# One table of places for every operation after the first batch, in a packed-attention and SoLU kernel

## Chip, cores and metric

The kernel runs on one core of a Trainium2 chip. The metric is the time of one execution on the device, in microseconds (us). TensorE is PE in the profile, VectorE is DVE, ScalarE is ACT, GpSimd is POOL, and SyncE is SP; SP only issues DMA requests here. The weight loads of PE have a row of their own, PEld.

## The reference: what is computed

Inputs are q, k and v with 8 batches, 8 heads, 576 rows and 64 columns, and p with 32 packing rows per head. All is fp32.

```python
def sm_attn(qq, kk, vv):
    s = scale * np.matmul(qq, kk.transpose(0, 1, 3, 2))
    s = s - np.max(s, axis=-1, keepdims=True)
    a = np.exp(s)
    a = a / (np.sum(a, axis=-1, keepdims=True) + 1e-09)
    return np.matmul(a, vv)
p_packed = sm_attn(p, k, v)
out = sm_attn(q, p_packed, p_packed)
...
h = x @ w_in                       # x: 4608 tokens x 512; w_in: 512 x 1024
e = np.exp(h - h_max)
sm = e / (np.sum(e, axis=-1, keepdims=True) + 1e-09)
solu = h * sm
ln = (solu - mu) / np.sqrt(var + 1e-06) * g_ln
return (ln @ w_out).astype(np.float32)      # w_out: 1024 x 512
```

x is the attention's output with the heads of a token side by side. So each batch first attends from 32 packing rows to its 576 keys, then from its 576 queries to the 32 packed rows, and then every token goes through a two-layer block with a SoLU and a layer norm between.

## The kernel before

**A batch's attention** has two halves. `pack(b)` (line 317) turns the keys on DVE (kT, line 325; for batch 0 on PE), multiplies them with p (line 343, two steps r for the even and the odd heads, each into two PSUM banks `pa`), takes the row maximum on DVE (lines 346, 348), the exponential on ACT (line 356), turns the result on PE (line 372) with copies by ACT (e1T, line 373), multiplies by v (line 382), divides (pp, line 386), and turns that once more (ppT, lines 388 and 390). `unpack(b)` (line 401) works out the scale (lines 407 to 411), turns q (line 419 on DVE; for batches 0 and 1 `transpose_rows` does it on PE, lines 128 and 130, with ACT copies), multiplies with ppT (line 458), and does the softmax over blocks of 32: DVE blocks and sums (lines 430, 434, 439 to 441), POOL subtraction and product (lines 435, 442), ACT exponential (line 437). It never multiplies by the packed rows at once: it forms z = packed rows times w_in (line 474), splits it into two fp16 parts zh and zl (lines 476, 482), and splits the attention weights likewise into a2h and a2l (lines 486 to 489).

**A token tile** is 128 tokens; there are 36, four and a half to a batch, so that every ninth one takes 64 tokens of each of two batches (two groups of half-height matmuls side by side). `mlp_in` (line 492) makes h from three fp16 products, 12 matmuls of 512 columns into a two-bank tile `h` of which there are two (line 512), then the row maximum nm, the bound and the bias on DVE (lines 514 to 523), the exponential on ACT (line 524), and u = e * s_row * h on DVE (line 527), after which the bank pair is free. `mlp_norm` (line 530) takes the mean on POOL (line 535), writes the two fp16 parts of y on ACT and DVE (lines 537, 538), has a DMA turn them (yT, line 540), and sums the squares on ACT (line 542); POOL makes the row factor (lines 544 to 548). `mlp_out` (line 551) is 24 matmuls of 512 columns into a bank `po` (line 557), evicted by ACT with the row factor (line 559) and stored by SP (line 564).

**PSUM's eight banks** are four for h, two for `po` and two for `pa`.

**The order.** Batch 0's attention and the weights' conversion (lines 203 to 219 for both weights, 305 and 306 for w_out's two fp16 parts wch and wcl) are put in order by the framework's scheduler with hand-set priorities; so are all engines but PE throughout. From batch 1 on PE follows the order in which the program is written (`manual_schedule`, line 619): `step` (line 600) writes a tile's first product, pieces of the attention of the batch one or two ahead (`more`, line 628, with counts in FIRST_BATCH and LATER), and an earlier tile's second product. The attention comes in 3 to 12 slots of a batch's tiles. SP's requests stand in one queue: for batch b + 2 the keys (4 requests), the values (3) and the queries (16 requests from `load_blocks`, line 80; for batch 1 the 4 requests of `load_rows`) are issued at the first tile of batch b. There are three input buffers `raw` for k and q, and one for v. `keep_busy` (line 246) puts matmuls on ones into a `po` bank, 22 of them on PE before the first key.

Of the kernel before, what the change touches and what calls it, by code (L numbers as in the profile page):

```python
# [19 lines left out]
A_TOP = 15  # L20
LOW_BY = 'aaaaaaaa'
ZL_BY = 'pppp'
A2L_BY = 'pppp'
B0_BY = 'pppp'
PACK0 = [-350, 400, 2010, 365, -1000, 60, -2800, 200, 200]
W_IN = [110, -3000, 100, 20]
UNPACK0 = [-80, 350, -35, -110, -70, -25, 1965, 1025, 0]
W_OUT = [190, 20, -50, 3010]
SCALE_AT = -1060
CHUNKS = [6, 0, 7, 5, 1, 3, 4, 2]  # L30
PARTS = [100, -1160, -990, -200, -3010, -1050, 200, 200]
FIRST_BATCH = [[0, 0, 1, 1, 1, 2, 0, 2, 0, 2, 0, 0], [0, 1, 0, 0, 0, 4, 1, 1, 0, 0, 1, 1], [3, 0, 6, 0, 0, 0, 0, 0, 0, 0, 0, 0], [1000, 375], [0, -400, -50], 190]
LOADS = 'wpkwvwwqooPoo'
BUSY = [[8, 100], [6, 0], [0, -3000], [0, -100], [2, -190], [0, -485], [4, 200], [2, -2885]]
LATER = [[[4, 0, 1, 0, 0, 0, 0, 0, 0, 0, 1, 1], [0, 1, 0, 0, 1, 0, 0, 1, 0, 2, 3, 1], [0, 0, 0, 0, 0, 0, 0, 0, 0, 0, 0, 0], [1000, -200], [0, -110, -200], 0], [[3, 1, 0, 0, 0, 1, 0, 0, 1, 0, 0, 1], [0, 0, 0, 0, 1, 0, 1, 1, 0, 2, 3, 1], [0, 0, 0, 0, 0, 0, 0, 0, 0, 0, 0, 0], [975, -200], [0, -100, -200], 0], [[4, 0, 1, 0, 0, 1, 0, 1, 0, 0, 0, 0], [0, 0, 2, 0, 1, 0, 0, 0, 0, 4, 2, 0], [0, 0, 0, 0, 0, 0, 0, 0, 0, 0, 0, 0], [1000, -200], [0, -110, -200], 0]]
FETCH = [[['k', 0, 0], ['v', 0, 0], ['q', 0, 0]], [['k', 0, 0], ['v', 0, 0], ['q', 0, 0]], [['k', 0, 0], ['v', 0, 0], ['q', 0, 0]]]
# [5 lines left out]
def packed_attention_solu_kernel(ctx: ExitStack, tc: tile.TileContext, q: bass.AP, k: bass.AP, v: bass.AP, p: bass.AP, w_in: bass.AP, w_out: bass.AP, g_ln: bass.AP, out: bass.AP):  # L42
# [34 lines left out]
    ps_o = ctx.enter_context(tc.tile_pool(name='ps_o', bufs=2, space=PSUM))  # L77
    ps_a = ctx.enter_context(tc.tile_pool(name='ps_a', bufs=2, space=PSUM))

    def load_blocks(dst, src):  # L80


        blocks = src.rearrange('(g r) (a t) (e i) -> r e t g a i', r=2, t=32, e=2)
        for g in range(G):
            for r in range(2):
                for e in range(2):
                    c = 2 * r + e
                    nc.sync.dma_start(dst[32 * c:32 * c + 32, g], blocks[r, e, :, g])

    def load_k(src):  # L90


        raw = raws.tile([P, G, NB, 32], F32, name='raw', bufs=3)
        dst = raw.rearrange('p g a i -> p (g a) i')
        blocks = src.rearrange('h (a n t) (e i) -> n e t (h a) i', n=2, t=32, e=2)
        for n in range(2):
            for e in range(2):
                c = 2 * n + e
                nc.sync.dma_start(dst[32 * c:32 * c + 32], blocks[n, e])
        return raw  # L100

    def load_x(src):
        raw = raws.tile([P, G, NB, 32], F32, name='raw', bufs=3)
        load_blocks(raw, src)
        return raw
# [211 lines left out]
    def pack(b):  # L317
# [58 lines left out]
        for r in range(2):  # L376
            for c in range(NSC):
                n = P if c < 4 else LEFT
                for g in range(G):
                    h = 2 * g + r  # L380
                    at = (c // 2 * H + h) * 128 + c % 2 * D if c < 4 else 2048 + h * D
                    nc.tensor.matmul(pav[32 * g:32 * g + 32, r * D:(r + 1) * D], lhsT=e1T[:n, 2 * c + r, 32 * g:32 * g + 32], rhs=v_sb[:n, at:at + D], start=c == 0, stop=c == NSC - 1)  # L382
            yield
        pp = att.tile([P, 2, D], F32, name='pp')
        for r in range(2):
            nc.vector.tensor_scalar_mul(pp[:, r], pav[:, r * D:(r + 1) * D], rs[:, r:r + 1])
        ppt = ps_a.tile([P, 512], F32, name='pa')
        nc.tensor.transpose(out=ppt[:, :P], in_=pp.rearrange('p r d -> p (r d)'), identity=ident)
        ppT = att.tile([P, P], F32, name='ppT', bufs=2)
        nc.vector.tensor_copy(ppT, ppt[:, :P])  # L390
        peak = small.tile([P, 1], F32, name='peak')
        nc.vector.tensor_reduce(out=peak, in_=pp.rearrange('p r d -> p (r d)'), axis=AX.X, op=ALU.max, apply_absolute_value=True)
        nc.tensor.matmul(ppt[:, P:P + 1], lhsT=ones_f, rhs=peak, start=True, stop=True)
        packed[b] = (ppT, ppt)
# [6 lines left out]
    def unpack(b):  # L401

        qraw = loaded.pop(('q', b))
        ppT, ppt = packed.pop(b)
        unit = units[b] = small.tile([P, 4], F32, name='unit', bufs=4)
        power = small.tile([P, 1], F32, name='power')
        nc.vector.tensor_scalar(out=power, in0=ppt[:, P:P + 1], scalar1=w_bound, scalar2=2.0 ** (-40), op0=ALU.mult, op1=ALU.max)
# [13 lines left out]
        eng = nc.gpsimd  # L421
# [3 lines left out]
        def scores(bank, r, n):  # L425
            rows = slice(64 * r, 64 * r + 64)
            return [(bank[32 * g:32 * g + 32, :HALF], ppT[rows, 32 * g:32 * g + 32], qT[rows, g, n * HALF:(n + 1) * HALF]) for g in range(G)]
# [4 lines left out]
        def softmax(r):  # L432
            mx = small.tile([P, NB], F32, name='mx')
            nc.vector.tensor_reduce(out=mx, in_=s2[r], axis=AX.X, op=ALU.max)  # L434
            eng.tensor_tensor(out=s2[r], in0=s2[r], in1=mx.unsqueeze(2).broadcast_to([P, NB, J]), op=ALU.subtract)  # L435
# [6 lines left out]
            eng.tensor_tensor(out=w2, in0=w2, in1=sm.unsqueeze(2).broadcast_to([P, NB, J]), op=ALU.mult)  # L442
# [10 lines left out]
        else:  # L453
            for n in range(2):
                banks = pair(b)
                for both in zip(*(scores(banks[r], r, n) for r in range(2))):
                    for out_, lhsT, rhs in both:
                        nc.tensor.matmul(out_, lhsT=lhsT, rhs=rhs, start=True, stop=True)  # L458
                for r in range(2):
                    blocks(banks[r], r, n)  # L460
                if n == 0:
                    yield
            for r in range(2):
                softmax(r)
# [3 lines left out]
        for n in range(2):  # L468
            banks = pair(b)
            cols = slice(512 * n, 512 * n + 512)  # L470
            for g in range(G):
                for r in range(2):
                    rows = slice(64 * r, 64 * r + 64)
                    nc.tensor.matmul(banks[r][32 * g:32 * g + 32, :], lhsT=ppT[rows, 32 * g:32 * g + 32], rhs=w_in_sb[rows, g, cols], start=True, stop=True)  # L474
# [9 lines left out]
        for r in range(2):  # L484
            a2T = att.tile([P, NB, J], F32, name='s2', bufs=2).rearrange('p a j -> p (a j)')
            nc.vector.transpose(out=a2T, in_=a2[r].rearrange('p a j -> p (a j)'))
            hi, lo = (a2h[b % 2][:, r], a2l[b % 2][:, r])
            nc.scalar.copy(hi, a2T)  # L488
# [3 lines left out]
    def mlp_in(row, parts):  # L492

        h = ps_h.tile([P, DF], F32, name='h')
        m = P // len(parts)
        groups = []
        for x, (i, c) in enumerate(parts):
            rows, cols = (slice(m * x, m * x + m), slice(c, c + m))
            terms = []
            for r in range(2):  # L500
                terms += [(rows, a2h[i][:, r, cols], zh[i], r), (rows, a2h[i][:, r, cols], zl[i], r), (rows, a2l[i][:, r, cols], zh[i], r)]
            groups.append(terms)
        last = len(groups[0]) - 1
# [178 lines left out]
```

## Time and profile before

| what | value |
|---|---|
| runs shown | 468.38, 467.36 and 465.05 us, median 467.36 |
| the profiled execution's own time | 464.53 us |
| its span, first to last instruction | 462.8 us |
| PE busy, all matmuls | 413.4 us, 89% of the span |
| DVE, ACT, POOL busy | 318.9, 253.1 and 140.3 us |
| first matmul of the first token tile | 53.1 us |
| first matmul of a second product (line 557) | 84.7 us |
| first product of the last tile ends | 442.6 us |
| DMA | 67.0 MB, of 237,880 packets 208,912 under 512 bytes |

A group row reads: line, engine, operation, output<-inputs, shapes, count, then the busy time and the mean of one in ns, then how long the engine stood idle before them and what ended that. A row of windows gives for a stretch its length, each engine's busy time with the number of its instructions, the granted share of PE's clock, the share of time that the DMA engines were busy, and GB/s. A row of waits gives who waited for whom, the total in us, how often, and the longest. A row of the timeline gives the start, the length, and in brackets the idle time before it. Matmuls overlap, so that the mean of one is longer than the step from one to the next; the chain, which counts each stretch once, shows 12 matmuls of 512 columns in 2.6 us.

### The profile page before, as it was taken

Reading aid. Unit: us, or ns where it says so; the run is one execution under the profiler, and the core shown is the slowest. Engines: PE = TensorE matmul, PEld = TensorE weight load, DVE = VectorE, ACT = ScalarE, POOL = GpSimd, SP = SyncE. Lnnn points to the kernel's source line nnn. Section 1 sums busy time; section 2 is a strip of 40 time slices with the busy share of each in tenths; the row PEclk is TensorE's granted clock in tenths of the full one; section 3 lists DMA queues with packets and bytes.
Section 4 is the critical chain, followed back from the end, with each engine's and each line's share of the span. In section 5 each row is a group of like instructions: output and inputs, shape, how many; then the busy total and the mean of one; then the engine's idle time right before and its main releaser. Section 6 shows DMA issues by size and latency. Waiting matters only on the chain.

```text
span 462.8 us, 8369 instructions
## 1 busy us (share of the span) xinstructions
PE 413.4 (89%) x3117; PEld 186.2 (40%) x3122; DVE 318.9 (69%) x651; ACT 253.1 (55%) x424; POOL 140.3 (30%) x274
## 2 busy tenths in 40 slices
PE   9795477978379999989799999999999999999996
PEld 7471233422233453435333453344334534444442
DVE  2469898774738786978479768876797678564540
ACT  3698646733504763566345663765456737446451
POOL 0003911344015222531145222613244245212220
PEclk9989589999657999999999999999999999999999
DMA  8999999996386289945946479235324322345223
GB/s 291 374 260 302 231 170 160 221 208 119 51 192 113 68 152 208 177 114 101 211 103 124 120 156 182 68 92 150 92 45 121 87 69 69 88 117 133 73 74 108
DMA packets 237880, 67.00 MB, mean 145 GB/s; under 512 B 208912, under 2 KB 231440, under 8 KB 237328
## 3 DMA queue, kind: packets, MB, share of 16 engines
q1 hardware_dynamic: 237840, 66.48, 63.0%
q8 instruction: 24, 0.39, 0.4%
q14 instruction: 16, 0.13, 0.1%
HBM read 37.23 MB, written 9.44 MB: 101 GB/s over the span
## 4 chain that ended last, share of the span: by engine, by line
PE 43%; DVE 29%; ACT 8%; issue 7%; DMA 6%; POOL 5%; SPq 2%; DVEq 0%; ACTq 0%; POOLq 0%
PE po L557 20%; PE h L512 9%; DVE kT L325 4%; DVE yhl L538 4%; DVE nm L514 3%; DMA yT<-yhl 3%; PE pa L382 3%; DVE qT L419 3%; PE pa L458 2%; DVE u L527 2%; DVE mx L346 2%; DMA v_sb<-in_v_dram 2%; ACT yhl L537 2%; PE pa L372 2%; ACT e L356 2%
## 5 line engine op out<-in xcount | busy, mean ns | idle before, releaser
L557 PE MATMUL po<-wch,yT 128*128 128x512 f16 x576 | 180.8, 382 | 5.9 <-DMA yT<-yhl 5.8
L557 PEld LDWEIGHTS <-yT 128*128 128x128 f16 x864 | 82.3, 99 | 117.3 <-issue 16.5
L557 PE MATMUL po<-wcl,yT 128*128 128x512 f16 x288 | 109.7, 381 | 0.0
L524 ACT ACTIVATE e<-h,bias,unit 128x1024 f32<-128x1024 f32 x36 | 43.3, 1202 | 59.3 <-DVE bias L523 47.4
L538 DVE SCALAR_TENSOR_TENSOR yhl<-u,negmu,yhl 128x1024 f16<-128x1024 f32 x36 | 47.0, 1306 | 27.6 <-ACT yhl L537 26.9
L512 PE MATMUL h<-zh,a2h 128*128 128x512 f16 (+1 forms) x160 | 58.7, 393 | 7.6 <-ACT a2h L488 7.6
L527 DVE SCALAR_TENSOR_TENSOR u<-e,s_row,h 128x1024 f32<-128x1024 f32 x36 | 45.8, 1271 | 22.5 <-ACT e L524 21.9
L512 PE MATMUL h<-zh,a2l 128*128 128x512 f16 (+1 forms) x160 | 59.2, 390 | 0.8 <-POOL a2l L489 0.6
L537 ACT ACTIVATE yhl<-u,negmu 128x1024 f16<-128x1024 f32 x36 | 41.4, 1149 | 32.2 <-POOL negmu L535 31.9
L512 PE MATMUL h<-zl,a2h 128*128 128x512 f16 (+1 forms) x160 | 58.1, 390 | 0.0
L514 DVE TENSOR_REDUCE nm<-h 128x1 f32<-128x1024 f32 x36 | 43.8, 1216 | 12.6 <-PE h L512 12.1
L512 PEld LDWEIGHTS <-a2h 128*128 128x128 f16 (+1 forms) x320 | 28.6, 102 | 47.5 <-issue 11.4
L544 POOL TENSOR_SCALAR s_eps<-se,s_row 128x1 f32<-128x1 f32 x36 | 9.8, 272 | 106.6 <-ACT e L524 70.9
L542 ACT ACTIVATE e<-u,negmu 128x1024 f32<-128x1024 f32 x36 | 40.8, 1134 | 0.0
L559 ACT ACTIVATE o_sb<-po,c_row 128x512 f32<-128x512 f32 x36 | 24.4, 678 | 28.7 <-PE po L557 28.7
L547 POOL TENSOR_SCALAR c_row<-sq,k_out,s_eps 128x1 f32<-128x1 f32 x36 | 14.5, 404 | 80.8 <-ACT e L542 80.6
L476 ACT ACTIVATE zh<-pa,unit 128x512 f16<-128x512 f32 x28 | 17.8, 682 | 29.1 <-PE pa L474 28.5
L435 POOL TENSOR_TENSOR s<-s,mx 128x576 f32<-128x576 f32 x16 | 22.0, 1393 | 34.0 <-DVE mx L434 34.0
L430 DVE STREAM_TRANSPOSE s<-pa 128x288 f32<-128x288 f32 x28 | 12.0, 463 | 23.5 <-PE pa L458 23.5
L372 PE MATMUL pa<-ident,e 128*128 128x128 f32 (+1 forms) x80 | 15.8, 319 | 10.8 <-ACT e L356 9.1
L512 PEld LDWEIGHTS <-a2l 128*128 128x128 f16 (+1 forms) x160 | 15.7, 102 | 21.3 <-POOL a2l L489 3.2
L442 POOL TENSOR_TENSOR a<-a,sm 128x576 f32<-128x576 f32 x16 | 18.3, 1156 | 17.2 <-DVE bound L517 6.9
(121 smaller groups left out, 562.6 us busy)
## 6 DMA issues: line engine op xcount, KB each, us to landing
out_dram<-o_sb SPq DMA_DIRECT2D x36, 256.0 KB, 2.6
v_sb<-in_v_dram SPq DMA_DIRECT2D x16, 512.0 KB, 5.6
raw<-in_k_dram SPq DMA_DIRECT2D x28, 288.0 KB, 4.6
raw<-in_q_dram SPq DMA_DIRECT2D x96, 72.0 KB, 2.5
zh<-in_moe_w_in_dram SPq DMA_DIRECT2D x2, 1024.0 KB, 5.6
zl<-in_moe_w_in_dram SPq DMA_DIRECT2D x2, 1024.0 KB, 7.3
raw<-in_q_dram SPq DMA_DIRECT2D x4, 512.0 KB, 7.7
raw<-in_moe_w_out_dram SPq DMA_DIRECT2D x2, 1024.0 KB, 6.1
```

The lines of the kernel that those rows point to most:

```text
L325: nc.vector.transpose(out=kT[:, g], in_=kraw[:, g].rearrange('p a i -> p (a i)'))
L372: nc.tensor.transpose(out=pt[:n, i * P:(i + 1) * P], in_=e1[:, r, cols], identity=ident)
L435: eng.tensor_tensor(out=s2[r], in0=s2[r], in1=mx.unsqueeze(2).broadcast_to([P, NB, J]), op=ALU.subtract)
L512: nc.tensor.matmul(h[rows, 512 * n:512 * n + 512], lhsT=lhsT, rhs=z[:, r, 512 * n:512 * n + 512], start=t == 0, stop=t == last)
L514: nc.vector.tensor_reduce(out=nm, in_=h, axis=AX.X, op=ALU.max, negate=True)
L524: nc.scalar.activation(e, h, AF.Exp, bias=bias, scale=unit[:, 1:2], accum_out=se)
L527: nc.vector.scalar_tensor_tensor(out=u, in0=e, scalar=s_row, in1=h, op0=ALU.mult, op1=ALU.mult, accum_out=su)
L537: nc.scalar.activation(yhl[:, 0], u, AF.Identity, bias=negmu)
L538: nc.vector.scalar_tensor_tensor(out=yhl[:, 1], in0=u, scalar=negmu, in1=yhl[:, 0], op0=ALU.add, op1=ALU.subtract)
L542: nc.scalar.activation(e, u, AF.Square, bias=negmu, accum_out=sq)
L557: nc.tensor.matmul(po, lhsT=yT[:, a, c], rhs=w[:, c], start=c == 0 and t == 0, stop=c == NFC - 1 and t == 2)
L559: nc.scalar.activation(o_sb, po, AF.Copy, scale=c_row)
```

## The change

**One table for all engines.** `pack` and `unpack` stay for batch 0 alone. For batches 1 to 7 (`attention`) and all 36 token tiles (`token_tile`) each operation is registered with a place in tiles: a tile's number, or 4.5 times the batch's, plus a number from the tables TILE, ATT and MORE (MORE holds other numbers for odd batches, batch 1, and tiles 0 to 5 and 33 to 35). `perform` sorts them, takes the first whose predecessors are done and whose buffers are free by its own count, and `issue` ties each engine's instructions to the one before it, so that PE, DVE, ACT, POOL and SP all keep this order. `step`, `mlp_in`, `mlp_norm`, `mlp_out`, `prefetch`, FIRST_BATCH, LATER and FETCH are gone; their instructions are the same in the new functions.

**What else differs.** Four `raw` requests of a q (line 910 of the changed file), each with its own place, replace 16, for batch 1 too, whose q is now turned on DVE. The packed rows are turned twice, into a ppT with both halves of the partitions filled (pp holds each twice), so that a half of q's rows is one softmax step. The sum of their peaks is copied out of PSUM by ACT (`total`). `pa` has 3 banks and `po` 1. In batch 0 the softmax's two POOL operations per step go to DVE, and so does one of four zl and one of two a2l; q's load is ahead of w_in's last two; the 22 matmuls on ones before the first key are gone, and 12 stand about the turning of the packed rows.

```diff
-LOADS = 'wpkwvwwqooPoo'
...
+NPA = 3
+NPO = 1
+TILE = {'m1': -0.05,
...
+LOADS = 'wpkvwqwwooPoo'
...
+    def perform():
+        left, done = (sorted(plan, key=lambda x: x[:2]), set())
+        while left:
+            for n, (_, _, at, fn, args, after, takes, gives) in enumerate(left):
+                if all(x.lstrip('~') in done or x.lstrip('~') not in known for x in after) and all(free[x] >= takes.count(x) for x in takes):
+                    break
...
+            issue(fn, args)
...
+    def issue(fn, args):
+        n = len(seen)
+        fn(*args)
+        for ins in nc.cur_bb.bb.instructions[n:]:
+            if ins.engine in last:
+                tc.add_manual_dep(ins, last[ins.engine], mybir.DependencyInfo(mybir.DependencyClass.NoSync, mybir.DependencyReason.DATA), reason='order')
+            last[ins.engine] = ins.name
...
+        def load_part(name, c):
+            blocks = src.rearrange('h (a n t) (e i) -> n e t (h a) i', n=2, t=32, e=2)
+            nc.sync.dma_start(st[name].rearrange('p g a i -> p (g a) i')[32 * c:32 * c + 32], blocks[c // 2, c % 2])
...
+        at('ex', row_exp, after=['nm'], takes='e')
+        at('u', solu, after=['ex', 'bd'], takes='u', gives='h')
+        at('tr', y_turn, after=['yl'], takes='yT', gives='y')
+        at('m2a', second, 0, after=['tr'], takes='po')
+        at('m2b', second, 1, after=['m2a'], gives='yT')
+        at('ev', output, after=['m2b', 'cr'], takes='o', gives='po')
```

On PE the table spreads a batch's attention over about seven tiles: scores, turning, value product, second scores and z stand singly between halves of second products. The first three tiles' first products stand in a row, in the order tile 2, 1, 0, then all of batch 1's attention up to the value product, and then the first second product, tile 0's.

On SP, at the first transposing request of a token tile (line 540 before, 1213 now), the queue stood so before:

```order
L99 DMA raw<-in_k_dram 32x72x32 x4
L88 DMA raw<-in_q_dram 32x18x32 x16
L99 DMA raw<-in_k_dram 32x72x32 x4
L540 DMA_TRANSPOSE yT<-yhl 128x16x128
L88 DMA raw<-in_q_dram 32x18x32 x2
```

and stands so now:

```order
L910 DMA raw<-in_k_dram 32x72x32 x2
L910 DMA raw<-in_q_dram 32x72x32 x2
L918 DMA v_sb<-in_v_dram 64x8x64
L910 DMA raw<-in_q_dram 32x72x32 x2
L1213 DMA_TRANSPOSE yT<-yhl 128x16x128 x2
```

Batch 2's q and batch 3's keys stood ahead of the first two transposes; now batch 1's rest and one part of batch 2's q do.

On DVE, where batch 2's first scores meet their row maxima (mx, line 346 before, 945 now; nm is a token tile's maximum, bias frees its exponential; kT, qT the turned inputs, zl and s parts of batch 1's attention), it was:

```order
L346 TENSOR_REDUCE mx_979<-pa 128x1 x2
L348 TENSOR_REDUCE nmx<-mx_979 128x1
L357 TENSOR_REDUCE ssum<-es 128x1
L514 TENSOR_REDUCE nm<-h 128x1
L346 TENSOR_REDUCE mx_998<-pa 128x1 x2
L325 STREAM_TRANSPOSE kT<-raw 128x576 x2
L516 TENSOR_SCALAR bound<-nm,unit_1234 128x1
L523 TENSOR_SCALAR bias<-nm,unit_1234 128x1
L325 STREAM_TRANSPOSE kT<-raw 128x576 x2
L348 TENSOR_REDUCE nmx<-mx_998 128x1
```

and is now:

```order
L1177 TENSOR_REDUCE nm<-h 128x1
L1179 TENSOR_SCALAR bias<-nm,unit 128x1
L945 TENSOR_REDUCE mx_1080<-pa 128x1 x2
L947 TENSOR_REDUCE nmx<-mx_1080 128x1
L1079 STREAM_TRANSPOSE s_1085<-a_1015 128x576
L1185 TENSOR_SCALAR bound<-nm,unit 128x1
L1186 TENSOR_SCALAR bound<-nm,bound 128x1
L1188 RECIPROCAL s_row<-bound 128x1
L1198 SCALAR_TENSOR_TENSOR u,su<-e,s_row,h 128x1024
L926 STREAM_TRANSPOSE qT<-raw 128x576
L945 TENSOR_REDUCE mx_1129<-pa 128x1 x2
L947 TENSOR_REDUCE nmx<-mx_1129 128x1
```

The next batch's kT stood between the second maximum and the nmx that the exponential waits for; now nmx follows its maximum, and those four kT stand 23 rows later.

On ACT, at a token tile without attention beside it (e,se the exponential, yhl the high part, e,sq the squares, o_sb the eviction of an older tile's second product), it was:

```order
L524 ACTIVATE e,se<-h,bias,unit 128x1024
L537 ACTIVATE yhl<-u,negmu 128x1024
L542 ACTIVATE e,sq<-u,negmu 128x1024
L559 ACTIVATE o_sb<-po,c_row 128x512
```

and is now:

```order
L1193 ACTIVATE e,se<-h,bias,unit 128x1024
L1236 ACTIVATE o_sb<-po,c_row 128x512
L1206 ACTIVATE yhl<-u,negmu 128x1024
L1217 ACTIVATE e,sq<-u,negmu 128x1024
```

The eviction has moved up to stand right behind the exponential of a tile two numbers higher, ahead of that tile's yhl; the squares behind it are now those of the tile before.

More of the change, by code (lines that the diff above doesn't have):

```diff
@@ L20 @@
 A_TOP = 15
[L21 to L32, printed above, removed]
@@ L425, in scores @@
         def scores(bank, r, n):
[L426 to L427 removed]
+            x = n if halves else r
+            rows = slice(64 * x, 64 * x + 64)
+            return [(bank[32 * g:32 * g + 32, :HALF], ppT[rows, r, 32 * g:32 * g + 32], qT[rows, g, (r if halves else n) * HALF:][:, :HALF]) for g in range(G)]
         def blocks(bank, r, n):
@@ L453, in unpack @@
         else:
-            for n in range(2):
+            for x in range(2):
                 banks = pair(b)
-                for both in zip(*(scores(banks[r], r, n) for r in range(2))):
+                which = [(x, y) if halves else (y, x) for y in range(2)]
+                for both in zip(*(scores(bank, *at) for bank, at in zip(banks, which))):
                     for out_, lhsT, rhs in both:
                         nc.tensor.matmul(out_, lhsT=lhsT, rhs=rhs, start=True, stop=True)
-                for r in range(2):
[L460 to L464, printed above, removed]
+                for bank, at in zip(banks, which):
+                    blocks(bank, *at)
+                if halves:
+                    softmax(x)
+                if x == 0:
+                    yield
+            if not halves:
+                for r in range(2):
+                    softmax(r)
             yield
@@ L551, in mlp_out @@
-    def mlp_out(row, yT, c_row, mid=None):
-        po = ps_o.tile([P, DM], F32, name='po')
-        for c in range(NFC):
-            if c == NFC // 2 and mid is not None:
-                mid()
-            for t, (a, w) in enumerate(((0, wch), (0, wcl), (1, wch))):
-                nc.tensor.matmul(po, lhsT=yT[:, a, c], rhs=w[:, c], start=c == 0 and t == 0, stop=c == NFC - 1 and t == 2)
-        o_sb = mlp.tile([P, DM], F32, name='o_sb', bufs=2)
-        nc.scalar.activation(o_sb, po, AF.Copy, scale=c_row)
-        stores.append((out[row:row + P, :], o_sb))
@@ L657 @@
+    for b in range(1, B):
+        attention(b)
+    for i in range(B * S // P):
+        token_tile(i)
+    with tc.high_priority(offset=AHEAD) if AHEAD else nullcontext():
+        perform()
 _INS = ['q', 'k', 'v', 'p', 'moe_w_in', 'moe_w_out', 'moe_g_ln']
```

879 lines of the change are left out of this document (714 added, 165 removed).

## The prediction, made before the changed kernel ran

> **What bounds the kernel now.** I read the page's busy rows and slices first, then PE's windows by stage, then its waits, then the chain.
>
> ```profile
> PE 413.4 (89%) x3117; PEld 186.2 (40%) x3122; DVE 318.9 (69%) x651; ACT 253.1 (55%) x424; POOL 140.3 (30%) x274
> PE   9795477978379999989799999999999999999996
> PEclk9989589999657999999999999999999999999999
> ```
>
> PE is the busiest engine, and its slices are full from the fourteenth on; the holes, and the clock's, lie before. So I cut the span where PE's work changes: first product begins (53), second products begin (84.7), clock back at full (144.3), last first product ends (442.6).
>
> ```profile
> core 0: us, PE busy (x) PEld busy (x) DVE busy (x) ACT busy (x) POOL busy (x), PEclk, DMA share, GB/s
> 0.00:53.00 53.00, 37.48 (x382) 24.37 (x387) 33.03 (x54) 35.50 (x58) 11.27 (x17) 0.92 1.00 298
> 53.00:84.70 31.70, 25.83 (x239) 12.82 (x240) 27.67 (x56) 20.11 (x41) 10.29 (x19) 0.86 1.02 177
> 84.70:144.30 59.60, 45.56 (x350) 17.37 (x349) 37.67 (x81) 22.54 (x39) 17.92 (x31) 0.77 0.76 152
> 144.30:442.60 298.30, 288.85 (x2080) 124.93 (x2079) 216.18 (x456) 169.47 (x279) 98.92 (x204) 1.00 0.52 115
> 442.60:462.80 20.20, 15.64 (x72) 6.74 (x70) 4.39 (x8) 5.52 (x8) 1.93 (x6) 0.96 0.36 104
> ```
>
> In the long stage PE is idle for 298.3 - 288.9 = 9.4 us: no order can take more than that there. In the third, the handover from batch 0 to batch 1, it is idle for 14.0 of 59.6 us and slow besides. In the first two DMA is busy all the time and DVE for 27.7 of 31.7 us. What PE waited for in the third and in the fourth stage:
>
> ```profile
> PE pa L372 <- ACT e L356: 5.0, 1, 5.0
> PE po L557 <- DMA yT<-yhl: 2.9, 1, 2.9
> PE pa L382 <- ACT e1T L373: 2.0, 1, 2.0
> ```
>
> ```profile
> PE po L557 <- DMA yT<-yhl: 2.9, 2, 2.4
> PE pa L343 <- DVE zl L482: 2.3, 2, 1.2
> PE pa L458 <- DVE ppT L390: 1.9, 5, 0.4
> ```
>
> The 5.0 us are the place of the DVE excerpt above: nmx stood behind four kT, and ACT's exponential behind nmx. The clock follows such stops:
>
> ```profile
> 99.30:102.70 3.40, 1.09 (x5) 0.51 (x6) 3.40 (x7) 0.86 (x2) 0.89 (x2) 1.00 1.22 274
> 102.70:106.10 3.40, 3.40 (x9) 1.18 (x8) 1.87 (x5) 0.68 (x1) 1.75 (x2) 0.50 0.83 163
> 119.75:143.64 23.89, 16.56 (x151) 7.11 (x152) 14.31 (x34) 7.95 (x16) 4.92 (x11) 0.50 0.70 139
> ```
>
> A window in which PE worked for 1.09 of 3.40 us is followed by half speed, and after the 5.0 us it lasted 23.9 us. Half of 16.56 and of 3.40 busy us, 8.3 + 1.7, is lost so: the handover holds 59.6 - 14.0 - 10.0 = 35.6 us of work at full speed. These are the durations that I use:
>
> ```profile
> 216.25 1.73 PE pa L382 x80
> ...
> 386.79 2.59 PE po L557 x12
> ...
> 400.86 2.59 PE h L512 x12
> ...
> 442.57 1.24 DVE nm L514
> ...
> 449.72 3.71 DMA yT<-yhl
> ```
>
> ```profile
> L524 ACT ACTIVATE e<-h,bias,unit 128x1024 f32<-128x1024 f32 x36 | 43.3, 1202 | 59.3 <-DVE bias L523 47.4
> L538 DVE SCALAR_TENSOR_TENSOR yhl<-u,negmu,yhl 128x1024 f16<-128x1024 f32 x36 | 47.0, 1306 | 27.6 <-ACT yhl L537 26.9
> L527 DVE SCALAR_TENSOR_TENSOR u<-e,s_row,h 128x1024 f32<-128x1024 f32 x36 | 45.8, 1271 | 22.5 <-ACT e L524 21.9
> ...
> L559 ACT ACTIVATE o_sb<-po,c_row 128x512 f32<-128x512 f32 x36 | 24.4, 678 | 28.7 <-PE po L557 28.7
> ```
>
> ```profile
> L325 DVE STREAM_TRANSPOSE kT<-raw 128x576 f32<-128x576 f32 x28 | 19.8, 749 | 0.0
> ...
> L439 DVE TENSOR_REDUCE sm<-a 128x18 f32<-128x576 f32 x16 | 11.7, 740 | 0.3 <-ACT a L437 0.2
> ...
> L306 DVE SCALAR_TENSOR_TENSOR wcl<-yhl,gs,wch 128x512 f16<-128x512 f32 x4 | 4.7, 1220 | 0.8 <-ACT wch L305 0.8
> ...
> L306 DVE SCALAR_TENSOR_TENSOR wcl<-yT,gs,wch 128x512 f16<-128x512 f32 x4 | 2.8, 741 | 0.0
> ```
>
> **The change, part by part.** *First token tile.* DVE reached the first nm at 65.61:
>
> ```profile
> 65.61 1.21 DVE L514 TENSOR_REDUCE nm<-h 128x1 f32<-128x1024 f32 x1
> ```
>
> Six operations come to DVE (four of the softmax, a zl, an a2l). The trace has none on DVE; the bounds are 0 each, if DVE waited anyway, and the 1.31 of a 128x1024 row; I take the 0.74 of L439, of their width: +4.4. The four kT of batch 1 now stand behind this nm: -2.7. Four of wcl took 1.22, the other four 0.74, 0.48 less: up to -1.9. The matmuls on ones about the packed rows put these, and all behind, off by some 2 (12 at their cold step of 0.43, half covered). I take 67.5, with 64 and 71 as ends. From there the new order makes a chain, tile 1 first. DVE: nm and bias 1.4, the exponential's 1.3, u 1.3 (now h is free, and tile 0's first product, the third in PE's list, runs), yhl from 5.7 to 7.0 as in the profile's last chain, four kT 2.7, tile 0's nm 1.4, batch 1's maxima 1.0, u at 13.9, its yhl at 16.7, the second maxima 1.0; then ACT's exponentials 1.2, ten turnings and a copy at half speed 3.1, and the value product at half speed, 2.9. That is 24.9: the first second product can begin at 92.4, for 84.7 now. Tile 2's first product is then done, tile 3's (2.6) is not. Batch 1's q costs PE no transposes any more; those (5.4) lay in waits of this stage and give nothing.
>
> In the Trainium skill's "TensorE: Matmul & The Clock Gate" (What's actually happening) the clock falls after an idle window of about 3.4 us. Here a window a third busy did it, so the measurement decides; by the page's rule alone the stops of this chain need not halve the clock, and the sum would be some 4 us less.
>
> *Handover.* 35.6 + 2.6 = 38.2 us of work. I laid the new lists of PE, DVE and ACT beside each other with these durations; PE stops for ppT (0.5, and 0.6 for batch 2), for `pa` banks of batch 1's second scores and z until DVE has read them (0.2, 0.95, 0.9, and 0.8 at batch 3's scores), for the second scores of batch 2, whose bank ACT's exponential frees behind a tile's (1.3), and for e1T (0.6): 5.9. Half speed for the first half of tile 0's second product: 1.3. With 14.0 as now it would be 8 more, with none 6 less. It ends 45.4 after 92.4: 137.8.
>
> *Long stage.* Its work is 288.9; the second turning of the packed rows adds 0.1 each, 0.8 in all with its copies hidden on DVE and ACT (busy 72% and 57% here). Nine tiles with two batches, laid out likewise from tile 9 on, give PE stops of 0.4 (ppT), 1.15 (scores, bank), 0.3 (z, bank) and some small ones: 2.7 for 9 tiles, against 98.0 - 92.8 = 5.2 now:
>
> ```profile
> 163.00:261.00 98.00, 92.81 (x720) 39.77 (x718) 73.88 (x160) 54.61 (x92) 33.08 (x65) 1.00 0.73 146
> ```
>
> Two and a half such periods have attention in them: 6.8, with 0 and 13 as ends. So 296.5. The single `po` bank costs nothing here: between two second products PE has a first product (2.6), and the eviction (0.68) stands behind an exponential that is over by then, unless DVE lags by more than 4 us.
>
> *SP.* The 16 requests of a q took 9.54, four of the same size 5.25:
>
> ```profile
> 72.81 5.25 SPq L99 DMA_DIRECT2D raw<-in_k_dram  x4
> ...
> 121.71 9.54 SPq L88 DMA_DIRECT2D raw<-in_q_dram  x16
> ```
>
> The packets are the same, so DMA is not relieved; only a transpose behind them lands sooner. The 2.9 + 2.9 us of PE's waits for yT are what that can be worth, and they are in the idle times above. Batch 1's q as 128-byte pieces falls in the stage where DMA is full; its last part waits for the kT to free a buffer and is wanted 9 us later: nothing.
>
> *Tail.* Three second products follow the last first product. The third eviction from the end now stands behind the last tile's exponential and yhl, 1.1 us after its product, and the next one costs 0.85; the 0.6 wait for yT is covered by that. 20.2 becomes 21.2 (20.2 to 22.2).
>
> **Sum.** 92.4 + 45.4 + 296.5 + 21.2 = 455.5 for 462.8, and 1.7 around it (464.53 - 462.8): 457. The three runs of before lie at 465.05 to 468.38, the profiled one half a us under them, so a run of after may come out up to 4 over the sum.
>
> **The rivals.** *Nothing is left to wait for:* the first nm as early as now (-2), half of the handover's stops (-3), none in the long stage (-6.8): 445. For it: DVE is busy for 73.88 of 98.0 us, and a spread attention asks for less at a time. Against: DVE's list is fixed, and its u and yhl rows show 22.5 and 27.6 us of waits. *The handover's loss comes back elsewhere:* one stop that drops the clock costs 8.3 as at 119.75: 465, no change. For it: my chain has two stops of 4 us for PE before 92. *DVE's order becomes the bound, slower:* per tile it has 73.88 / 9 = 8.2 us of work and waits of (22.5 + 27.6) / 36 = 1.4; PE's pace is 10.6. From 1 us more of waiting per tile, DVE sets the pace; at 2 us more, 1 us per tile over the 22 tiles left: 479. For it: pp, ss and zl now stand in the list as single places, each behind PE or ACT. Against: my nine tiles, where they waited for 2.3, 0.7 and nothing.
>
> Another way to be slower is in the skill's section on a second failure mode (psum-queue depth-cycling), same page: micro-stops between groups with cycled PSUM banks make the clock oscillate. Here stops of up to 2.4 us left it at 1.00 through 298 us; it is in the slower case with 0.02.
>
> That the order isn't kept is no rival: the lists are the program.
>
> **How the numbers follow.** Forecast (449 to 463) 0.45, nothing left to wait for 0.24, no change 0.18, slower 0.13. About 1% can be told from no change. Faster by over 1% is below 462.7: the second case and nearly all of the first, 0.68; same 0.19; slower 0.13. The range reaches to the rivals' middles without the slowest: 443 to 469; the forecast's own is 449 to 463.
>
> **What would show it.** Right: the first nm at 66 to 69, the first second product at 90 to 95, half speed before it and none after 105; PE idle under 4 us per nine tiles from 140 on; no PE wait over 2 us there. Wrong: second products before 86 or after 98; DVE without idle time in the long stage; PE waits for `po`.

## The result, and the profile after

The changed kernel takes 434.58 us (median of 4 runs, 432.99 to 435.57), the kernel before 467.87 beside it (465.05 to 468.69): a ratio of 0.9295, 95% interval 0.9242 to 0.9348. The direction was forecast; the size, 457, and the range, 443 to 469, were not: the kernel is 8 us faster than the range's lower end. The profiled execution has a span of 431.9 us. Of the kernel with PE and SP alone tied (below) one execution took 801.08 us beside 476.74 to 482.78 in three others; it is not explained, and the ratio given for that kernel leaves it out.

The busy row and two slices of the profile after:

```profile
PE 388.8 (90%) x3053; PEld 179.5 (42%) x3053; DVE 331.3 (77%) x662; ACT 247.7 (57%) x422; POOL 135.3 (31%) x268
...
PE   7697075499999999999999999999999999999985
...
PEclk9999668699999999999999999999999999999999
```

From the ninth slice on PE is full, but for the last two, and its granted clock (PEclk, in tenths) stays at full. PE's windows of the changed kernel, cut at the same events as before: first product begins (56.0), second products begin (87.8), the fourth second product begins (127.9), the last first product ends (410.2); then nine tiles of the long stage, and the two middle stages as one:

```profile
core 0: us, PE busy (x) PEld busy (x) DVE busy (x) ACT busy (x) POOL busy (x), PEclk, DMA share, GB/s
56.00:87.80 31.80, 19.74 (x159) 8.82 (x160) 25.06 (x45) 17.45 (x32) 6.78 (x14) 0.71 0.51 91
87.80:127.90 40.10, 38.34 (x347) 17.00 (x344) 33.87 (x78) 20.91 (x38) 14.39 (x26) 1.00 0.90 174
127.90:410.20 282.30, 279.55 (x2104) 124.43 (x2103) 230.13 (x471) 169.05 (x286) 104.15 (x207) 1.00 0.64 137
410.20:431.90 21.70, 15.84 (x72) 6.84 (x70) 4.51 (x8) 6.27 (x10) 3.37 (x10) 1.00 0.46 110
...
170.20:259.10 88.90, 88.19 (x719) 39.52 (x718) 75.83 (x160) 54.02 (x94) 33.83 (x67) 1.00 0.81 159
...
87.80:410.20 322.40, 317.89 (x2450) 141.43 (x2447) 264.00 (x548) 189.96 (x324) 118.55 (x232) 1.00 0.68 142
```

| | before | forecast | after |
|---|---|---|---|
| first nm | 65.6 | 67.5 | 64.0 |
| first second product begins | 84.7 | 92.4 | 87.8 |
| handover, to the fourth second product | 59.6 | 45.4 | 40.1 |
| long stage | 298.3 | 296.5 | 282.3 |
| tail | 20.2 | 21.2 | 21.7 |
| span | 462.8 | 455.5 | 431.9 |

Of the miss of 23.6 us 4.6 lie ahead of the first second product, 5.3 and 14.2 in the two middle stages, and the tail gives 0.5 back. All that PE still waits for between 87.8 and 410.2:

```profile
PE pa L1010 <- DVE ppT L1007: 3.5, 5, 0.9
PE pa L940 <- DVE s L1035: 0.6, 1, 0.6
PE pa L1028 <- DVE s L1035: 0.2, 1, 0.2
```

To see where the 35 us of these stages went, I take both as one stretch, from the start of the first second product to the end of the last first product. Before, its row is this:

```profile
84.70:442.50 357.80, 334.31 (x2427) 142.28 (x2426) 253.82 (x535) 192.00 (x318) 116.75 (x235) 0.96 0.56 122
```

Length less PE's busy time is idle time: 23.5 before, 4.5 after. From the records I also add the steps from each matmul of the attention to the next matmul, without the idle time that the trace shows, apart for the stretches at half speed. Before, 20.2 us of steps of all kinds lie at half speed, so 10.1 are lost; after, almost none. The attention's steps come to 64.3 us before, with those at half speed counted half, and to 56.8 after. So 35.4 is 19.0 of idle time, 10.1 of half speed and 7.5 of the attention's steps, less about 1 in the steps of the two products (one first product more, 2.6, lies in the stretch after). The last part was a surprise: the matmuls are the same, but for one more turning. By line it is the second scores that fell most, from 15.8 us (line 458) to 9.4 (line 1028); the first scores fell by 1.7, the turning of e by 1.7, and z rose by 1.2. The table, used for the experiments too, holds one profiled execution of each kernel; the attention column counts half speed in full, and for the kernel before with 3 + 1 banks it holds 1.7 of matmuls on ones, which write an attention bank there:

| kernel | stretch begins | its length | PE idle in it | attention's steps |
|---|---|---|---|---|
| before | 84.7 | 357.8 | 23.5 | 70.6 |
| after | 87.8 | 322.4 | 4.5 | 56.8 |
| after, 2 + 1 banks | 93.4 | 354.0 | 20.1 | 67.0 |
| after, 2 + 2 banks | 92.2 | 353.4 | 19.6 | 67.2 |
| before, 3 + 1 banks | 93.7 | 343.4 | 20.3 | 61.5 |
| after, PE and SP tied | 94.7 | 357.5 | 27.4 | 62.2 |
| after, PE, SP and DVE tied | 90.5 | 326.0 | 5.9 | 56.9 |
| after, groups split | 88.5 | 332.0 | 4.7 | 66.1 |
| after, control of that | 88.8 | 323.5 | 3.9 | 58.5 |
| before, PE tied | 84.6 | 361.9 | 28.3 | 69.8 |

### The profile page after: what moved, and what is told of

The parts are those of the page before. It is cut to its first block, busy times and chain, and to the rows that moved or that the text cites. A ratio compares the mean times of both kernels' runs of the same rounds, so it can differ in the third digit from the quotient of the medians.

```text
span 431.9 us, 8093 instructions
## 1 busy us (share of the span) xinstructions
PE 388.8 (90%) x3053; PEld 179.5 (42%) x3053; DVE 331.3 (77%) x662; ACT 247.7 (57%) x422; POOL 135.3 (31%) x268
## 4 chain that ended last, share of the span: by engine, by line
PE 75%; DVE 10%; ACT 5%; issue 4%; SPq 3%; DMA 2%; POOL 1%; ACTq 0%; DVEq 0%
PE po L1232 41%; PE h L1173 19%; PE pa L1066 4%; PE pa L991 3%; PE pa L940 2%; PE pa L974 2%; PE pa L1028 2%; DVE u L1198 2%; DMA zh<-in_moe_w_in_dram 2%; SPq L449 1%; ACT yhl L1206 1%; DVE yhl L1209 1%; SPq L441 1%; DVE nm L1177 1%; PE pa L581 1%
## 5 line engine op out<-in xcount | busy, mean ns | idle before, releaser
L1173 PE MATMUL h<-zh,a2h 128*128 128x512 f16 (+1 forms) x160 | 56.4, 391 | 12.1 <-ACT a2h L835 7.8
L1209 DVE SCALAR_TENSOR_TENSOR yhl<-u,negmu,yhl 128x1024 f16<-128x1024 f32 x36 | 45.6, 1265 | 23.7 <-ACT yhl L1206 23.7
L1173 PE MATMUL h<-zh,a2l 128*128 128x512 f16 (+1 forms) x160 | 55.9, 387 | 0.3 <-POOL a2l L836 0.3
L1173 PE MATMUL h<-zl,a2h 128*128 128x512 f16 (+1 forms) x160 | 55.9, 387 | 0.0
L1206 ACT ACTIVATE yhl<-u,negmu 128x1024 f16<-128x1024 f32 x36 | 41.3, 1147 | 19.6 <-POOL negmu L1202 19.2
L1202 POOL TENSOR_SCALAR negmu<-su 128x1 f32<-128x1 f32 x36 | 6.8, 190 | 89.0 <-DVE u L1198 84.9
L1224 POOL TENSOR_SCALAR c_row<-sq,k_out,s_eps 128x1 f32<-128x1 f32 x36 | 15.7, 436 | 47.4 <-ACT e L1217 46.0
L1094 POOL TENSOR_TENSOR a2l<-s,a2h 128x576 f16<-128x576 f32 x14 | 18.8, 1343 | 29.4 <-ACT a2h L1090 29.4
L1042 POOL TENSOR_TENSOR s<-s,mx 128x576 f32<-128x576 f32 x14 | 17.2, 1227 | 26.5 <-DVE mx L1039 26.5
L1055 POOL TENSOR_TENSOR a<-a,sm 128x576 f32<-128x576 f32 x14 | 18.6, 1332 | 19.6 <-DVE sm L1052 19.6
L955 ACT ACTIVATE e<-pa,nmx 128x288 f32<-128x288 f32 x28 | 13.7, 494 | 19.1 <-DVE nmx L947 19.1
L1046 ACT ACTIVATE a<-s 128x576 f32<-128x576 f32 x14 | 9.5, 682 | 24.6 <-POOL s L1042 24.6
```

The lines of the kernel that those rows point to most:

```text
L1055: nc.gpsimd.tensor_tensor(out=st['a2', r], in0=st['a2', r], in1=st['sm', r].unsqueeze(2).broadcast_to([P, NB, J]), op=ALU.mult)
L1094: nc.gpsimd.tensor_tensor(out=lo, in0=a2T, in1=hi, op=ALU.subtract)
L1173: nc.tensor.matmul(h[rows, 512 * n:512 * n + 512], lhsT=lhsT, rhs=z[:, r, 512 * n:512 * n + 512], start=t == 0, stop=t == end)
L1206: nc.scalar.activation(st['y'][:, 0], st['u'], AF.Identity, bias=st['negmu'])
L1209: nc.vector.scalar_tensor_tensor(out=st['y'][:, 1], in0=st['u'], scalar=st['negmu'], in1=st['y'][:, 0], op0=ALU.add, op1=ALU.subtract)
```

## The experiments

Times are medians, ratios are to the kernel before beside the same runs (the changed kernel's own is 0.9295).

### Is it the third attention bank?

In two kernels the bank counts of the changed kernel are other ones: two for the attention and two for the second product, as before; then two and one, so that the attention's count alone differs. `perform` counts free banks, so that it also places some operations later: with two and one banks, of the order of lines that PE worked through, 190 of 206 entries stand as they did, and of DVE's 477 of 522.

```diff
-NPA = 3
-NPO = 1
+NPA = 2
+NPO = 2
```

> The changed kernel with two banks for the attention and two for the second product, as before (the table is the same; the planner moves the few rows that do not fit). Theory 'the third attention bank took the bank waits away': PE waits for DVE to read scores and z, about 1 us per batch and more at the handover: 440 to 448. Rival 'the banks do not matter, the order does': 434 to 437.

> The changed kernel with two attention banks in place of three and one bank for the second product, as it has now (seven of the eight banks used). Theory 'the third attention bank is what the table needs': as with two and two, 463 to 472. Rival 'it was the second bank of the second product that moved the order for the worse': 434 to 442.

Measured: 467.54 (ratio 1.0024, 0.9992 to 1.0056) and 466.91 (1.001, 0.9981 to 1.0038). The whole gain is gone with one attention bank less, far more than the 440 to 448 that I had expected of the first kernel, and whether the second product has two banks or one makes no difference beside it. Of the 37.2 us by which the span grew 5.7 lie ahead of the first second product. PE's windows and waits of the kernel with two and one:

```profile
93.40:447.40 354.00, 333.95 (x2450) 144.89 (x2447) 265.31 (x547) 189.59 (x324) 113.88 (x232) 0.97 0.62 129
...
141.30:144.70 3.40, 1.45 (x17) 0.31 (x16) 3.23 (x11) 0.66 (x2) 0.73 (x3) 1.00 0.82 163
144.70:151.50 6.80, 6.18 (x40) 1.81 (x39) 4.34 (x11) 2.43 (x6) 2.36 (x3) 0.50 0.45 93
```

```profile
PE pa L1066 <- ACT e L955: 6.4, 2, 3.2
PE pa L1028 <- DVE s L1035: 3.6, 4, 1.7
...
PE pa L1066 <- ACT e1T L981: 2.3, 3, 1.3
PE pa L940 <- DVE s L1035: 1.8, 3, 0.6
```

The rows of waits name what PE waits for: a bank that ACT's exponential or its copy, or DVE's transpose, has not read yet. z (line 1066) stands in PE's list between other operations' banks, and with two of them it stands until one is read. Behind a window with 1.45 busy us of 3.40, the clock is at half for 6.8. And the timeline of PE shows what such a wait does to a group of eight matmuls that needs two banks:

```profile
167.78 1.04 PE L1066 MATMUL pa<-w_in_sb,ppT 64*32 64x512 f32 x2
170.14 1.09 PE L1066 MATMUL pa<-w_in_sb,ppT 64*32 64x512 f32 x14 [1.32 <-ACT e1T L981]
```

Each fp32 matmul has two records. The first of the eight found its bank free and ran alone for 1.04 us; the other seven waited 1.32 more, and then took 1.09 together, as long as all eight take in a row. So the wait cost 1.32 of idle time and some 1.04 that the profile counts as busy.

Then the other way round: the kernel before with three attention banks and one for the second product, nothing else of the change (its matmuls on ones write an attention bank).

```diff
-    ps_o = ctx.enter_context(tc.tile_pool(name='ps_o', bufs=2, space=PSUM))
-    ps_a = ctx.enter_context(tc.tile_pool(name='ps_a', bufs=2, space=PSUM))
+    ps_o = ctx.enter_context(tc.tile_pool(name='ps_o', bufs=1, space=PSUM))
+    ps_a = ctx.enter_context(tc.tile_pool(name='ps_a', bufs=3, space=PSUM))
```

> The kernel before with three banks for the attention and one for the second product, and nothing else of the change (the matmuls on ones write an attention bank). Theory 'the third attention bank is the gain by itself': PE's bank waits and the pairs that stood apart go as they did in the changed kernel, some 20 us or more less, 440 to 450. Rival 'the third bank is worth something only with lists that use it': the old lists have kT, sums and maxima in places that make DVE late anyway, and the single bank of the second product now waits for its eviction: 462 to 472.

Measured: 461.73 (0.9895, 0.9859 to 0.993). Neither number: a little is gained. The table tells why: the stretch is 14.4 us shorter, but begins 9.0 later and leaves a tail of 24.5 for 20.3. The late start lies in batch 0: the first product of a token tile begins at 62.1 for 53.1, behind a wait of 11.5 us for a2h that was 6.2. In the stretch PE now waits for the second product's bank:

```profile
PE po L558 <- ACT o_sb L560: 6.7, 5, 1.8
PE po L558 <- DMA yT<-yhl: 5.9, 4, 2.4
```

Of the stretch, the bank alone takes 14.4, the table alone (two and one banks) 3.8, both 35.4; of the whole time they take 5, nothing and 33. Most of the gain needs the two together. Why batch 0 came later is open.

### Which engines' lists?

The same table, but only some engines are tied to it, and the scheduler orders the rest.

```diff
         for ins in nc.cur_bb.bb.instructions[n:]:
+            if ins.engine not in (mybir.EngineType.PE, mybir.EngineType.SP):
+                continue
             if ins.engine in last:
```

> The changed kernel with only PE and SP tied to the table's order; the scheduler orders DVE, ACT and POOL. Theory 'the fixed lists of DVE, ACT and POOL took the waits away': PE's idle time of 0.7 us per nine tiles goes back towards the 5.2 of before, some 13 us over the long stage, and the first 88 us change too: 445 to 460. Rival 'PE's order alone does it': within 2 us of 434.6.

> The same kernel as with PE and SP alone tied, for a profile to read: 477 to 483; the theories differ in the place: if the scheduler's order of DVE is at fault, PE's idle time ends at DVE's nm, maxima and transposes, if ACT's, at its exponentials and evictions.

> The changed kernel with PE, SP and DVE tied to the table's order; the scheduler orders ACT and POOL alone. Theory 'DVE's list is the one that matters', since most of PE's waits end at DVE: 434 to 442. Rival 'ACT's list matters as much' (the eviction ahead of yhl, the exponentials): 455 to 485, as with PE and SP alone (482).

Measured: 482.45 with PE and SP alone (median of all four; 1.0274, 1.0198 to 1.0349), slower than before by 2 to 3.5%; 476.8 in the execution whose profile stands below; 440.38 with DVE tied too (0.9428, 0.9395 to 0.9461). DVE's list, added to those of PE and SP, is worth 36 to 42 us, and those of ACT and POOL on top of it 5.8. The windows of PE's stretch and its waits with PE and SP alone, then the windows with DVE tied too:

```profile
94.70:452.20 357.50, 330.08 (x2449) 143.86 (x2446) 256.98 (x539) 187.34 (x320) 116.26 (x228) 0.97 0.60 128
```

```profile
PE pa L1068 <- ACT e L957: 4.7, 2, 2.4
PE pa L942 <- ACT e L957: 4.6, 1, 4.6
PE pa L942 <- DVE s L1037: 4.2, 1, 4.2
PE pa L1030 <- DVE s L1037: 4.0, 3, 2.5
PE po L1234 <- ACT o_sb L1238: 3.6, 3, 2.2
```

```profile
90.50:416.50 326.00, 320.06 (x2449) 141.63 (x2446) 262.68 (x543) 188.81 (x322) 120.40 (x230) 1.00 0.67 140
```

The place is again a bank that waits for a reader, in the last row the second product's: line 957 is the attention's exponential, which stands behind DVE's maxima, line 1037 DVE's transpose of the second scores. With DVE in the table's order 27.4 us of idle time become 5.9. In these runs three banks are enough only where DVE reads them in the order in which PE fills them.

### What is a group of eight worth?

A transposing matmul of the unit matrix, into columns that nothing reads, behind the first of the eight matmuls of each second-score group; as a control, the same one behind the eighth.

```diff
                     nc.tensor.matmul(bank[y][32 * g:32 * g + 32, :HALF], ...)
+                    if g == 0 and y == 0:
+                        nc.tensor.transpose(out=bank[y][:, HALF:HALF + P], in_=ident, identity=ident)
```

> The changed kernel with one transposing matmul of the unit matrix (128 columns, into columns of the same bank that nothing reads) put behind the first of the eight quarter matmuls of each second-score group, 14 groups in all. Theory 'whole groups': the eight run side by side and cost 0.65 us together, the first one alone costs 0.60 (the rows of before at 176.88 and 221.16), so each group grows by 0.60 and the added 0.12: 14 x 0.72 = 10 us, nearly all on PE's path, 444. Rival 'PE has slack': the group's cost is hidden and only the added matmul counts or nothing does: 434.6 to 436.5.

> The control: the same transposing matmul, but behind the eighth of each group, so that the groups stay whole. Theory 'whole groups': 14 x 0.12 = 1.7, so 436.3. Rival 'an added matmul with a wait costs as much wherever it stands': as the split kernel, 444.

Measured: 443.32 (0.9486, 0.9433 to 0.9538) and 435.9 (0.932, 0.9282 to 0.9359), 8.7 and 1.3 over the changed kernel, where 10 and 1.7 were expected. The split itself is the difference, 7.4 us or 0.53 for each of 14 groups; the attention's steps differ by 66.1 - 58.5 = 7.6. One group in PE's timeline, whole in the changed kernel, then split:

```profile
177.33 0.72 PE L1028 MATMUL pa<-qT,ppT 64*32 64x288 f32 x16
177.98 0.39 PE L1232 MATMUL po<-wch,yT 128*128 128x512 f16 x1
```

```profile
181.63 0.67 PE L1028 MATMUL pa<-qT,ppT 64*32 64x288 f32 x2
182.24 0.33 PE L1030 MATMUL pa<-ident 128*128 128x128 f32 x1
182.49 0.71 PE L1028 MATMUL pa<-qT,ppT 64*32 64x288 f32 x14
183.13 0.39 PE L1234 MATMUL po<-wch,yT 128*128 128x512 f16 x1
```

Whole, the next line begins 0.65 after; split, 1.50: the first of eight alone holds PE for 0.61, as long as all eight side by side. The kernel before has such groups all along, by the scheduler (221.16) or by a bank (201.94, 1.30 to the next line, with no foreign matmul in it, so that the loss needs no change of shape):

```profile
201.94 1.37 PE L343 MATMUL pa<-kT,pT 64*32 64x288 f32 x16 [1.23 <-DVE zl L482]
203.24 0.39 PE L512 MATMUL h<-zh,a2h 128*128 128x512 f16 x1
...
221.16 0.67 PE L458 MATMUL pa<-qT,ppT 64*32 64x288 f32 x2 [0.38 <-DVE ppT L390]
221.76 0.38 PE L393 MATMUL pa<-peak,ones_f 128*128 128x1 f32 x2
```

In the Trainium skill's "TensorE: Matmul & The Clock Gate" (Part 3: Packing small matmuls) small matmuls at different places of the array run at the same time, in a span of about one of them. The trace agrees, 0.65 for eight beside 0.61 for one; that a group loses this when its second bank is late, only these runs show.

Is the split a cause by itself in the kernel before? There PE alone was tied to its written order, which puts the second scores' groups together.

```diff
+                if last and link:
+                    tc.add_manual_dep(ins, last[0], ..., reason='order')
```

> The kernel before with PE alone tied to its written order from the sixth tile on, which only puts the groups of second scores together again that another line's matmul had split (some 8 of them). Theory 'whole groups': 8 x 0.6 = 5 us less, 463 for 467.9. Rival 'before is set by its waits': the 5 us come back as idle time of PE, 467 to 469.

Measured: 468.43 (1.0019, 0.9995 to 1.0044). My theory fell here: idle time rose from 23.5 to 28.3, and the attention's steps fell by 0.8 only (by 2.3 with half speed counted half), because about half of the groups, now whole in the list, stop inside for a bank:

```profile
180.05 0.72 PE L458 MATMUL pa<-qT,ppT 64*32 64x288 f32 x16
181.40 1.08 PE L458 MATMUL pa<-qT,ppT 64*32 64x288 f32 x16 [0.63 <-DVE s L430]
```

The kernel before with 3 + 1 banks, still in the scheduler's order, tells the rest. Of the 14 groups of second scores ten have another line's matmul inside them in the kernel before and one has there; 13 take 0.65 us or less, and their lines' steps fall from 15.8 us to 8.8. So the split groups are how a scarce bank shows, not a second cause beside it.

### One row on DVE, and SP's requests

Batch 3's four kT back ahead of batch 2's second maximum, as they stood before, and their last two requests earlier on SP, by moving entries of the finished list (each named part to ahead of the mark):

```diff
+MOVES = [('lk2/3 lk3/3', 'lv2/2'), ('kt0/3 kt1/3 kt2/3 kt3/3', 'mx1/2')]
...
+        for names, mark in MOVES:
+            part = [x for n in names.split() for x in order if x[0] == n]
+            order[:] = [x for x in order if x not in part]
+            at = [x[0] for x in order].index(mark)
+            order[at:at] = part
```

and a q's four requests cut into sixteen:

```diff
+            for x in range(4 if name == 'q' else 1):
+                n = G * 18 // 4 if name == 'q' else G * 18
+                nc.sync.dma_start(st[name].rearrange('p g a i -> p (g a) i')[32 * c:32 * c + 32, n * x:n * x + n], ...)
```

> The changed kernel with batch 3's four kT put back ahead of batch 2's second row maximum on DVE (as they stood before), and its last two key requests that much earlier on SP. Theory 'one row on DVE makes the handover's stop and the clock's': batch 2's exponential comes 2.7 us later, PE stands for about 2.6 us after tile 4's first product (near 117), and what follows runs at half speed for 3.4 us or more: 2.6 + 1.7 to 2.6 + 8 longer, 439 to 445. Rival 'DVE's slack takes it': under 1 us, 434 to 436.

> The changed kernel with each of a q's four requests cut into four, at the same places in SP's queue. Theory 'order, not number, of the requests': the transposes of y still land in time, 434 to 436. Rival 'SP's issue time counts': 16 requests hold SP 4.3 us longer per batch (9.54 against 5.25), and PE waits for yT again as it did before, 2.9 us in the handover and 2.9 later: 438 to 441.

Measured: 437.08 (0.9365, 0.931 to 0.942) and 435.07 (0.9324, 0.9263 to 0.9385). The misplaced kT make the expected stop, and no half speed:

```profile
118.87:121.27 2.40, 0.01 (x2) 0.01 (x1) 2.37 (x7) 1.07 (x4) 0.00 (x0) 1.00 0.59 100
121.27:131.90 10.63, 9.72 (x134) 5.43 (x135) 9.85 (x24) 8.16 (x13) 2.81 (x7) 1.00 0.54 130
...
116.90:120.31 3.41, 1.98 (x17) 0.86 (x13) 3.38 (x9) 0.86 (x2) 0.34 (x1) 1.00 0.71 158
120.31:123.73 3.42, 2.41 (x53) 1.82 (x57) 3.28 (x7) 2.70 (x8) 0.00 (x0) 1.00 0.52 81
```

2.5 us more for a stop of 2.4: here it costs itself, and not the 8.3 that I gave one stop in the second rival. That may be its place: the granted clock of this run changes in steps of 3.41 us (at 72.52, 79.34 and 89.58, say), and on that grid the stop lies across two windows, in which PE still works for 1.98 and 2.41 us. The number of q's requests makes no difference that can be told.

### The start and the tail

PE stands for 4.83 us in the first chain. Tile 1's second product was moved there (its y transposed first); then the same with its eviction behind the third tile's exponential instead of ahead of it, and the last tile but one's second product in an attention bank; then also with the third tile's y earlier; and the tail's edit alone.

```diff
+MOVES = [('tr-1', 'lq0/2'), ('m2a-1 m2b-1', 'tp0/1'), ('ev-1', 'm2a-0')]
```

```diff
+MOVES = [('tr-1', 'lq0/2'), ('m2a-1 m2b-1', 'tp0/1'), ('nm-2 bd-2 ex-2 ev-1', 'm2a-0')]
...
+                st['po'] = ps_a.tile([P, DM], F32, name='pa') if i == 34 else ps_o.tile([P, DM], F32, name='po')
```

```diff
+MOVES = [('tr-1', 'lq0/2'), ('m2a-1 m2b-1', 'tp0/1'), ('nm-2 bd-2 ex-2 ev-1', 'm2a-0'), ('yh-2 yl-2 tr-2', 'pk/1')]
```

> The changed kernel with tile 1's second product (5.2 us) moved from behind tile 0's to the hole of 4.83 us that PE has before batch 1's turning (77.9 to 82.9), its y transposed first and evicted at once. Theory 'PE's time is the limit from 88 on': what is done in the hole is gained, 4 to 5 us, 430 to 431. Rival 'the chain on DVE and ACT is the limit until 128, and the product is missed later as a filler', or the product runs at half speed and takes the gain back: 434 to 437.

> The changed kernel with tile 1's second product in PE's hole at 78, its eviction this time behind the third tile's exponential, and the second product of the last tile but one in an attention bank. The tail gives 1.1 to 1.4 as it did alone. Theory 'the eviction's place took the gain': 3 to 4 us on top, 429 to 430. Rival 'the chain on DVE and ACT up to 108 is the limit, whatever PE does in the hole': 433.

> As before, and the third tile's two parts of y moved ahead of the scale's operations on ACT and DVE, and their transpose ahead of batch 2's requests, so that its second product is there when PE asks for it (it waited 3.4 us for it). Theory 'PE's time from 88 on': 2 to 3 us less than without, 427 to 429. Rival 'DVE's list is full there, and what is put ahead is missed behind': no less than without.

> The changed kernel with the second product of the last tile but one in an attention bank, which is free by then. Theory 'the single po bank costs the tail its two stops' (1.16 and 0.78, each behind an eviction): 1.9 less, 432.7. Rival 'the last eviction waits for its own factor and nothing is gained': 434.6.

Measured: 434.18 (0.9302, 0.9238 to 0.9366), 433.48 (0.9281, 0.9257 to 0.9304), 434.88 (0.9328, 0.9302 to 0.9355) and, the tail alone, 433.2 (0.9287, 0.9258 to 0.9316). The second products begin at 77.9 instead of 87.8 in the first of them, and nothing comes of it: tile 3's nm begins at 108.16 in the changed kernel,

```profile
108.16 1.18 DVE L1177 TENSOR_REDUCE nm<-h 128x1 f32<-128x1024 f32 x1
```

and at 108.83, 108.99 and 110.26 in the three. PE's time comes back as waits, in the first of them for a yT (with 3.4 us at half speed behind it), in the third for DVE (waits from 76 to 130):

```profile
PE po L1240 <- DMA yT<-yhl: 3.4, 1, 3.4
...
PE pa L948 <- DVE zl L1083: 1.9, 1, 1.9
PE pa L948 <- DVE kT L934: 1.0, 1, 1.0
```

So the time up to there is set by the chain on DVE and ACT, as the rival had it; no run makes that chain shorter. The tail's two stops in the changed kernel, for the single second-product bank, and what is left with the edit:

```profile
416.51 0.38 PE L1232 MATMUL po<-wch,yT 128*128 128x512 f16 x1 [1.16 <-ACT o_sb L1236]
...
422.63 0.38 PE L1232 MATMUL po<-wch,yT 128*128 128x512 f16 x1 [0.78 <-ACT o_sb L1236]
```

```profile
420.31 0.39 PE L1232 MATMUL po<-wch,yT 128*128 128x512 f16 x1 [0.48 <-DMA yT<-yhl]
```

1.94 less 0.48 is 1.5; the stage itself is 20.65 for 21.71, 1.1 less, and the median is 1.4 lower. The intervals overlap, so that the trace shows this and the times alone do not.

## Why the prediction was wrong, step by step

**"No order can take more than that there"** is the step that failed: the 9.4 us of idle time in the long stage were taken as all that can be gained, and its 288.9 us of busy time as work. The stage fell by 16.0, its busy time to 279.6. Over the whole stretch 7.5 us of the attention's busy time were no work, most of them waits in disguise: groups of scores that ran apart, broken by another line's matmul or held inside by a late bank (6.4 in the second scores, 1.7 in the first; the rest nearly cancels). In nine tiles PE's busy time fell from 92.81 to 88.19 us with two batches in them; 1.1 of that is the window's edge (five matmuls of a second product more before), and 3.3 the attention. The Trainium skill's "Perfetto Trace Analysis" (Identifying the Most-Contended Engine) says that the matmuls' busy share is no good measure of how close a kernel is to its limit; these rows agree, by 3.3 us of 92.8, but not for the page's reason, which is that pipelined instructions look smaller.

**The third bank had no term.** I listed 3 + 1 banks among the changes, asked what the single second-product bank would cost and found nothing (right in the middle, 1.9 in the tail), and never asked what the third attention bank would give. It decides: 466.91 without it, though alone it gave 461.73.

**The stops were oversized.** Laid out by hand, PE's stops came to 5.9 in the handover and 6.8 later; 1.8 and 2.8 were measured. Those for ppT in the handover (0.5 and 0.6, measured 0.52 and 0.86) and for the second scores (0.2, measured 0.2) were about right, and the 0.8 at batch 3's scores measured 0.6. Those for z and for ACT's exponential (0.95, 0.9, 1.3) and e1T (0.6) did not come. Stops 8.2, half speed 1.3, and 10.0 of what I took for work make the 19.5 us by which the two stages' 341.9 missed 322.4.

**The first tile** came 3.5 before the forecast. DVE is busy for 45.2 us ahead of nm, and was for 44.8 before: the six operations that came to it took the place of the four kT and of slow wcl, about as the sum had it, but its idle time fell by 2.0, from 20.9 to 18.8, which only the lower end of my bounds, 64, allowed for. The 2 us for matmuls on ones are not seen in nm's time, though the first product itself begins 2.9 later (56.0 for 53.1). The chain behind it took 23.8 for 24.9, with the two PE stops of over 4 us and half speed that ends with the first second product, as forecast. But its end is not what the later stages stand on: with that product at 77.9 the rest did not move.

**SP** was right: four requests for sixteen are worth nothing that can be told (435.07 with sixteen). The waits for yT, 5.2 us before, are gone, as the idle times had it.

**The tail** was forecast at 21.2 and is 21.7, by the evictions named.

**The rivals.** The nearest was "nothing left to wait for", at 445 with 0.24: its reason, DVE's slack, is near what happened, but it too counted idle time alone, and gave 22 of the 33 us that came. "DVE's order becomes the bound" did not come in this table, but it is a danger in kind: with DVE, ACT and POOL left to the scheduler the same kernel takes 476.7 to 482.8. Oscillation of the clock by micro-stops between banks is not seen after (1.00 from 87.8 to 410.2); with two attention banks and one the clock did fall in the stretch, three times for 6.8 us, each behind a window with 1.1 to 1.5 busy us of 3.4.

**The signs.** The first nm (64.0) and the first second product (87.8) lie outside the marks for right; the clock after 105 (1.00), PE's idle time in nine tiles (0.7) and its longest wait there (0.9) lie inside. PE did wait for `po`, in the tail alone (1.9).

## What to carry to other kernels

Before taking PE's busy time as a floor, look at one group of its small matmuls in the timeline: if the step to the next line differs between two groups of the same shape (0.65 and 1.30 here), the difference is a wait that no idle time shows. Where a matmul engine fills buffers that others empty, count the buffers and follow the emptying order together: here a bank alone was worth 14.4 us of the stretch and 5 of the whole time, the order alone 3.8 and nothing, both 35.4 and 33. And a stop that is filled with other work is a gain only where the engine filled is the one that sets the time; the later tile's nm, not the first second product, told which.

## What the runs showed of the hardware

Eight fp32 matmuls of 64 rows and 32 columns on 288 columns take 0.65 us in a row, and one of them alone 0.61. A wait of 2.4 us left the granted clock at 1.00 (121.27 to 131.90 above) where the two 3.4 us windows about it had 1.98 and 2.41 busy us, while a 3.4 us window with 1.45 busy was followed by half speed for 6.8 us.
